# Own tiles for the first pairs' squares and key halves, another order of their factors, 24 turns of the identity, and a changed rule for when the planner lets loads follow each other

## The chip, the core and the metric

The kernel runs on one core of a Trainium2 chip. The time is in device microseconds (us) from start to end of one execution. Five instruction streams work at once: TensorE (PE in the profile, with its weight loads as PEld), VectorE (DVE), ScalarE (ACT), GpSimd (POOL) and SyncE (SP), which here only issues DMAs. Each runs its own instructions in the order in which the program lists them; they wait for each other at semaphores.

## What is computed

Attention with normalized queries and keys over 8 x 12 heads of 448 positions and 64 dimensions, and a two-layer product with a cosine between the layers on its output:

```python
def rmsnorm(x, g):
    rms = np.sqrt(np.mean(x * x, axis=-1, keepdims=True) + 1e-06)
    return x / rms * g
q_n, k_n = (rmsnorm(q, g_q), rmsnorm(k, g_k))
scores = scale * np.matmul(q_n, k_n.transpose(0, 1, 3, 2))
scores = scores - np.max(scores, axis=-1, keepdims=True)
attn = np.exp(scores)
attn = attn / (np.sum(attn, axis=-1, keepdims=True) + 1e-09)
attn_out = np.matmul(attn, v).astype(np.float32)
...
x = np.ascontiguousarray(attn_out.transpose(0, 2, 1, 3)).reshape(B * S, H * D)
h = x @ w_in          # 3584 x 768 by 768 x 2048
g = h * np.cos(h)
return (g @ w_out).astype(np.float32)
```

## The kernel before

The 96 heads are handled as 48 pairs `u`, two heads on the 128 partitions, and six pairs make one batch of 448 tokens (`NP = 6`, eight batches). For each pair the kernel computes the scores (`score`, L425), the row minimum (the sign of the scores is turned, `rowmin`, L443), the exponential with its row sums (`expo`, L453), transposes of the result on TensorE (`transp`, L480), and the product with the values (`av_whole` L516 for the first nine pairs, `av` L506 for the others). Four score tiles fit into PSUM for the first batch (three in ring `S`, one in `ph`). The hidden layer of a batch (`ffn1`, L564) is multiplied in among the attention of the next batch, and its result goes through SBUF tiles `he` (two of them) to a buffer `h_d` in DRAM (`h_out` L583, `h_store` L587).

The weights of the first layer come as 64-bit floats in 16 loads of 768 KB (`w_load`, L202). VectorE and ScalarE decode them (`decode`, L210), ScalarE and GpSimd split them into a high and a low part. The second layer's weights are decoded too, combined, and kept in DRAM as `wo_d`.

**The first two pairs** (`NFIRST = 2`) are prepared in a shorter way than the others (`first`, L737). The two halves of `sd` (queries `c = 0`, keys `c = 1`) are loaded (`first_load`, L309), squared on ScalarE into the PSUM tile `pt` (`first_square`, L313), summed on VectorE (`first_reduce`, L318) and raised to the power -1/2 on GpSimd (`st_pow`, L304). The keys are multiplied by their factor (`first_norm`, L326), turned on TensorE into `pt` (`first_turn`, L332), and copied into the tile `khi`, its upper half by ScalarE and its lower by VectorE (`first_keys`, L337). The queries are scaled by GpSimd with a constant that VectorE makes out of the small load `gs` (`q_scale` L382, `g_fold` L189), and their own factor is multiplied in by the row minimum (L449). `pt` is also what all transposes go through.

**What sets the order.** No engine's order is written by hand. Each step is handed to `Plan.add` with its engine, an assumed cost, a due time, what it reads and writes, for DMAs an assumed time `land` until the data is there, and sometimes an earliest time `start`. `Plan.order` (L69) runs a list scheduler over these assumed times: when an engine is free, it takes the step with the earliest due time among those that are ready. The result is one fixed list; on the chip each engine works through its part of it, whatever the real times are, and the assumed times are not waited for. Rings (`RING` L196, `RING2` L892) are tiles with several copies: the first user of copy n waits in the plan for all users of copy n - ring size, and (L73) for the first user of copy n - 1. If that first user is a DMA, the plan counts its cost, its `land` and a signal time of 0.16 before the next may start.

**The second part** (from L890) has a plan of its own. It starts with the hidden layer of the last batch in 16 blocks of 3.66 us (`ffn1_block`, L577), and beside it prepares the blocks of the second layer: `gl_load` (L593) loads two rows of `h_d` into `hb` (three copies), ScalarE and VectorE compute the cosine (L599 to L623), VectorE or GpSimd adds or subtracts blocks (`g_mix`, L625), ScalarE and GpSimd split them (`g_split`, L628), and TensorE multiplies them with the weights that `v_place` (L277) loads (`ffn2`, L637). For each of four pairs of batches there are 16 such blocks, in four groups g for each of the roles a, b, d, c; seven products follow in order, the first with a, the second with b (made of d and b).

Of the kernel before, what the change touches and what calls it, by code (L numbers as in the profile page):

```python
# [27 lines left out]
class Plan:  # L28
# [9 lines left out]
    def __init__(self, rings):  # L38
        self.rings = rings
        self.parts = []  # L40
        self.start = []
        self.lead = []
        self.writer = {}
        self.readers = {}
        self.users = {}

    def add(self, eng, cost, due, fn, *args, r=(), w=(), land=0.0, start=0.0, lead=None):
# [21 lines left out]
    def order(self):  # L69
        parts = self.parts  # L70
        for (name, inst), users in self.users.items():
            parts[users[0]][5].update(self.users.get((name, inst - self.rings[name]), ()))
            parts[users[0]][5].update(self.users.get((name, inst - 1), ())[:1])  # L73
            parts[users[0]][5].discard(users[0])
            for n in users[1:]:
                parts[n][5].add(users[0])
# [14 lines left out]
        while True:  # L91
            best = None
            for e in free:
                if can[e]:
                    t = free[e]
                elif wait[e]:
                    t = max(free[e], wait[e][0][0])
                else:
                    continue
                if best is None or t < best[0]:  # L100
                    best = (t, e)
            if best is None:
                break
            t, e = best
            while wait[e] and wait[e][0][0] <= t:
                n = heapq.heappop(wait[e])[1]
                heapq.heappush(can[e], (parts[n][2], n))
            n = heapq.heappop(can[e])[1]
            cost, fn, args, land = (parts[n][i] for i in (1, 3, 4, 6))
            end = free[e] = t + cost  # L110
            self.busy[e] += cost
            seq.append((t, n, fn, args))
            for m in after[n]:
                same = parts[m][0] == e and not land
                gap = 0.0 if same else land + self.SIGNAL + self.lead[m]
                ready[m] = max(ready[m], end + gap)
                left[m] -= 1
                if not left[m]:
                    heapq.heappush(wait[parts[m][0]], (ready[m], m))
# [7 lines left out]
def tile_attention_moe(  # L127
# [185 lines left out]
    def first_square(u, c):  # L313
        nc.scalar.activation(
            pt[:, 512 * (1 - c) : 512 * (1 - c) + S], pair[u][f"sd{c}"].rearrange("p t d -> p (t d)"), AF.Square
        )

    def first_reduce(u, c):  # L318
        if c:
            tl(u, "r", [128, 14], F32)  # L320
        src = pt[:, 512 * (1 - c) : 512 * (1 - c) + S].rearrange("p (t d) -> p t d", d=D)
        r = pair[u]["r"][:, 7 * c : 7 * c + 7]
        nc.vector.tensor_reduce(r, src, axis=AX.X, op=ALU.add)
        nc.vector.tensor_scalar(r, r, 1.0 / D, 1e-6, op0=ALU.mult, op1=ALU.add)  # L324

    def first_norm(u):  # L326
# [3 lines left out]
        del pair[u]["sd0"]  # L330

    def first_turn(u):  # L332
        kn = pair[u].pop("rkb")
        for t in range(7):
            nc.tensor.transpose(pt[:D, t * 128 : t * 128 + 128], kn[:, t * D : t * D + D], ident)

    def first_keys(u, hh):  # L337
        if hh == 0:
            tl(u, "khi", [128, S], F32)
        dst = pair[u]["khi"][64 * hh : 64 * hh + 64].rearrange("d (p t) -> d t p", t=7)  # L340
        src = pt[:D, :896].rearrange("d (t c) -> d t c", c=128)[:, :, 64 * hh : 64 * hh + 64]
        if hh == 0:
            nc.scalar.copy(dst, src)  # L343
        else:
            nc.vector.tensor_copy(dst, src)
# [79 lines left out]
    def score(u, j):  # L425
# [5 lines left out]
        for n, t in enumerate(tiles):  # L431
            tag = place(u, 2 * j + n)[0]
            pool = ps_h if tag == "ph" else ps_s
            d["S", t] = pool.tile([128, 512], F32, tag=tag, name=f"S{u}_{t}")
        for n, (a, c) in enumerate(ops):
            for t in tiles:
# [263 lines left out]
    def weights(fc):  # L700
        d = ffn_due(0, 3 * fc) - 6.0
        w, f = ("w", fc), ("wf", fc)
        begin = (4.0, 7.0, 20.0)[fc] if fc < 3 else max(24.0 + 7.0 * fc, d - WAHEAD)
        add(SP, ISS, d - 30.0, w_load, fc, w=[w if f64 else f], land=8.0, start=begin)
# [32 lines left out]
    def first(u):  # L737
        D0 = base(u) - 34.0
        add(SP, 2 * ISS, D0, first_load, u, w=[("P", 2 * u), ("P", 2 * u + 1)], land=2.6)
        for c in (1, 0):  # L740
            z = [("pt", 0, 1 - c)]
            add(ACT, 0.5, D0 + 2 - c, first_square, u, c, r=[("P", 2 * u + 1 - c)], w=z)
            add(DVE, 0.75, D0 + 3 - c, first_reduce, u, c, r=z, w=[("r", u, c)])
            add(POOL, 1.5, D0 + 4 - c, st_pow, u, 7 * c, 7 * c + 7, w=[("r", u, c)])
        add(DVE, 0.65, D0 + 5, first_norm, u, r=[("P", 2 * u), ("P", 2 * u + 1), ("r", u, 1)], w=[("rkb", u)])
        z = [("pt", 0, 0), ("pt", 0, 1)]
        add(PE, 1.2, D0 + 6, first_turn, u, r=[("rkb", u)], w=z, lead=0.0)
        add(ACT, 0.6, D0 + 7, first_keys, u, 0, r=z, w=[("khi", u, 0)])
        add(DVE, 0.65, D0 + 7, first_keys, u, 1, r=z + [("khi", u, 0)], w=[("khi", u, 1)])
        add(SP, ISS, D0 + 1, q_load, u, w=[("qd", u)], land=4.0)  # L750
        add(POOL, 0.8, D0 + 5, q_scale, u, r=[("gsc", 0), ("qd", u), ("r", u, 0)], w=[("qhi", u)])
        add(SP, ISS, base(u) - 6, v_whole, u, w=[("vs", u, 0)], land=LAND, start=14.0 + 6 * u)

    def prepare(u):
# [25 lines left out]
        for hh in range(2):  # L780
            vd, vs = [("vd", 2 * u + hh)], [("vs", u, hh)]
            add(SP, ISS, D0 - 12 + 6 * hh, v_load, u, hh, w=vd, land=LAND)
            add(POOL, 0.56, D0 + 6 * hh, v_high, u, hh, r=vd, w=vs)
            add(POOL, 0.91, D0 + 2 + 6 * hh, v_low, u, hh, r=vd, w=vs)

    def attend(u):
# [4 lines left out]
        for j in range(4):  # L791
# [4 lines left out]
            operands = ("qhi", "khi") if u in S32 else ("qhi", "ql", "khi", "kl")  # L796
            add(PE, cost, dj, score, u, j, lead=lead, r=[(n, u) for n in operands if u >= NFIRST or n != "khi"] + ([("khi", u, 0), ("khi", u, 1)] if u < NFIRST else []), w=keys)
            for t, key in zip(tiles, keys):
# [11 lines left out]
        for kc in range(4):  # L810
# [14 lines left out]
            for hh in range(2):  # L825
                n = 8 * u + 2 * kc + hh
                eng, cost = (DVE, 0.62) if u in A32 and hh and kc < 3 else (ACT, 0.53)
# [8 lines left out]
            if u in A32:  # L836
                n = 8 * u + 2 * kc
                add(PE, 1.0, dk + 4, av_whole, u, kc, lead=lead, r=[("vs", u, 0), ("hi", n), ("hi", n + 1)], w=[("O", u, 0)])
                continue
            for hh in range(2):  # L840
                n, m = 8 * u + 2 * kc + hh, 6 * u + 2 * kc + hh
                r = [[("hi", n), ("lo", m)], [("hi", n), ("lo", m)], [("lo", m)], [("hi", n), ("hi", n - 2)]][kc]
# [16 lines left out]
    def multiply(b):  # L859
        for fc in range(NFC):  # L860
# [7 lines left out]
            add(SP, ISS, d, h_store, b, fc, r=[("he", NFC * b + fc)], land=LAND)  # L868

    for u in range(NP):  # L870
        (first if u < NFIRST else prepare)(u)
# [191 lines left out]
```

## Time and profile before

| | |
|---|---|
| median of three runs | 1447.98 us (1443.79, 1447.98, 1448.81) |
| the profiled execution | 1448.93 us |
| its span, from the first to the last instruction | 1447.1 us |
| mean granted TensorE clock | 0.998 |
| HBM read, written | 218.24 MB, 62.89 MB |

Everything in the profile belongs to one execution; it ran 1.8 us longer than its span and 0.95 us longer than the median run. Where a row is a line of the time line, it gives start, duration, engine, line of the kernel, operation, output<-inputs and, in brackets, how long the engine had been idle and what ended that. In a row of the windows, each engine has its busy time and its number of instructions, then come the granted clock, the busy share of the DMA engines and GB/s. An fp32 product stands in the records as two matmul instructions.

### The profile page before, as it was taken

What the parts mean: (1) busy time and instruction counts of PE and PEld (TensorE: products, weight loads), DVE (VectorE), ACT (ScalarE), POOL (GpSimd) and SP (SyncE); (2) the same over time, 40 slices, a digit from 0 to 9 for tenths busy, and PEclk for the clock granted to TensorE, in tenths of its full rate; (3) what the DMA queues carried; (4) which work ended last, traced back from release to release, by engine and by line L of the source; (5) the groups of instructions that cost most, each with busy time, mean ns of one, the idle gap of its engine ahead of it and who ended that gap; (6) DMA issues with size and microseconds to landing.
All of it is one profiled execution on the core that took longest, in us unless ns stands there. A gap on an engine that the chain in (4) does not pass through costs nothing.

```text
span 1447.1 us, 22426 instructions
## 1 busy us (share of the span) xinstructions
PE 1397.0 (97%) x7361; PEld 1152.7 (80%) x7361; DVE 1020.8 (71%) x1649; ACT 1001.6 (69%) x2058; POOL 932.6 (64%) x722
## 2 busy tenths in 40 slices
PE   6999999999999999999999999999999999999998
PEld 2445687888888788787878788889889899899898
DVE  6878885677778777869676755536876876977821
ACT  5777677677777777777776676547676776786742
POOL 5678777566877867787884673101295596585684
PEclk9999999999999999999999999999999999999999
DMA  6788444555667576566654542149569569489373
GB/s 207 230 259 255 129 129 133 151 175 173 192 200 222 166 219 206 185 206 188 215 184 159 163 149 87 55 132 347 195 201 327 188 224 338 154 265 339 124 238 101
DMA packets 154452, 282.62 MB, mean 195 GB/s; under 512 B 31760, under 2 KB 102368, under 8 KB 154336
## 3 DMA queue, kind: packets, MB, share of 16 engines
q1 hardware_dynamic: 154336, 281.20, 60.7%
q8 instruction: 58, 0.95, 0.3%
q14 instruction: 58, 0.48, 0.1%
HBM read 218.24 MB, written 62.89 MB: 194 GB/s over the span
## 4 chain that ended last, share of the span: by engine, by line
PE 71%; DVE 14%; ACT 5%; DMA 4%; issue 4%; POOL 2%; SPq 0%; ACTq 0%; DVEq 0%; POOLq 0%
PE ph L573 9%; PE PT L483 8%; PE ph L574 8%; PE ph L575 8%; PE O L514 8%; PE S L438 7%; PE y L649 7%; PE y L650 7%; PE y L648 7%; DVE lo L502 2%; DMA hb<-h_d 2%; ACT hi L494 1%; POOL glo L633 1%; DVE sm L447 1%; PE O L522 1%
## 5 line engine op out<-in xcount | busy, mean ns | idle before, releaser
L573 PE MATMUL ph<-xs,wi 128*128 128x448 f32 x768 | 299.2, 390 | 1.5 <-ACT he L585 1.5
L574 PE MATMUL ph<-xs,wi 128*128 128x448 f32 x768 | 281.1, 366 | 0.0
L575 PE MATMUL ph<-xs,wi 128*128 128x448 f32 x768 | 281.0, 366 | 0.0
L456 ACT ACTIVATE P<-S,sm 128x448 f32<-128x448 f32 x336 | 213.7, 640 | 78.7 <-DVE sm L447 66.6
L649 PE MATMUL y<-glo,wo 128*128 128x448 f32 x672 | 247.1, 368 | 7.3 <-POOL glo L633 7.3
L648 PE MATMUL y<-ghi,wo 128*128 128x448 f32 x672 | 246.8, 367 | 0.3 <-ACT ghi L635 0.3
L650 PE MATMUL y<-ghi,wo 128*128 128x448 f32 x672 | 246.7, 367 | 0.0
L494 ACT CAST hi<-PT 128x448 fp32r<-128x448 f32 x312 | 153.5, 536 | 93.9 <-PE PT L483 49.6
L447 DVE TENSOR_REDUCE sm<-S 128x1 f32<-128x448 f32 x322 | 186.7, 611 | 25.6 <-PE S L438 24.9
L483 PEld LDWEIGHTS PT<-ident,P 128*128 128x128 f32 x1344 | 155.5, 141 | 41.6 <-issue 22.8
L502 DVE TENSOR_TENSOR lo<-PT,hi 128x448 fp32r<-128x448 f32 x234 | 134.7, 617 | 71.5 <-ACT hi L494 70.2
L483 PE MATMUL PT<-ident,P 128*128 128x128 f32 x1344 | 181.2, 275 | 3.0 <-DVE hi L492 3.0
L573 PEld LDWEIGHTS ph<-xs,wi 128*128 128x128 f32 x768 | 144.5, 188 | 34.9 <-issue 15.7
L575 PEld LDWEIGHTS ph<-xs,wi 128*128 128x128 f32 x768 | 144.2, 188 | 12.6
L574 PEld LDWEIGHTS ph<-xs,wi 128*128 128x128 f32 x768 | 144.9, 189 | 9.7 <-issue 0.4
L649 PEld LDWEIGHTS y<-glo,wo 128*128 128x128 f32 x672 | 126.6, 188 | 19.4 <-POOL glo L633 8.7
L306 POOL TENSOR_TENSOR r<-r,nhalf 128x14 f32<-128x14 f32 (+1 forms) x50 | 128.5, 2570 | 12.5 <-DVE r L324 8.9
L648 PEld LDWEIGHTS y<-ghi,wo 128*128 128x128 f32 x672 | 126.6, 188 | 11.7 <-ACT ghi L635 0.7
L650 PEld LDWEIGHTS y<-ghi,wo 128*128 128x128 f32 x672 | 126.6, 188 | 10.9
L438 PE MATMUL S<-khi,qhi 64*128 64x448 f32 x399 | 115.0, 518 | 1.7 <-ACT khi L343 1.2
L514 PE MATMUL O<-hi,vs 128*128 128x448 f32 x312 | 101.9, 381 | 7.3 <-ACT hi L494 3.3
L514 PE MATMUL O<-lo,vs 128*128 128x448 f32 x234 | 89.3, 397 | 10.3 <-DVE lo L502 9.8
(225 smaller groups left out, 2710.7 us busy)
## 6 DMA issues: line engine op xcount, KB each, us to landing
wo<-wo_d SPq DMA_DIRECT2D x88, 768.0 KB
h_d<-he SPq DMA_DIRECT2D x128, 224.0 KB
hb<-h_d SPq DMA_DIRECT2D x64, 448.0 KB
wo_d<-wv SPq DMA_DIRECT2D x56, 384.0 KB
sd<-sd SPq DMA_DIRECT2D x46, 448.0 KB
vd<-v SPq DMA_DIRECT2D x78, 160.0 KB
qd<-qT SPq DMA_DIRECT2D x48, 256.0 KB
raw<-w_in SPq DMA_DIRECT2D x16, 768.0 KB
```

The lines of the kernel that those rows point to most:

```text
L438: nc.tensor.matmul(d["S", t][:, :S], d[a][p0:p1, j * 128 : j * 128 + 128], d[c][p0:p1, :], start=(n == 0), stop=(n == len(ops) - 1),)
L447: nc.vector.tensor_reduce(least, d["S", t][:, :S], axis=AX.X, op=ALU.min)
L456: nc.scalar.activation(tl(u, f"P{t}", [128, S], F32, "P"), d.pop(("S", t))[:, :S], AF.Exp, bias=sm[:, 1, t : t + 1], scale=-1.0, accum_out ...
L483: nc.tensor.transpose(pt[:, t * 128 : t * 128 + 128], src, ident)
L494: nc.scalar.copy(hi, pt[:, hh * S : hh * S + S])
L514: nc.tensor.matmul(O, st, d.pop((what, kb, hh)), start=(kc + n == 0), stop=(kc + n == 4))
L573: nc.tensor.matmul(ph[:, :S], whi, x2[:, 0, :], start=(cc == 0), stop=False)
L574: nc.tensor.matmul(ph[:, :S], whi, x2[:, 1, :], start=False, stop=False)
L575: nc.tensor.matmul(ph[:, :S], wlo, x2[:, 0, :], start=False, stop=(cc == NCC - 1))
L648: nc.tensor.matmul(y, whi, hi, start=(k == 0 and chain < 2), stop=False, skip_group_check=chain == 2)
L649: nc.tensor.matmul(y, whi, lo, start=False, stop=False, skip_group_check=chain == 2)
L650: nc.tensor.matmul(y, wlo, hi, start=False, stop=(k == NH - 1), skip_group_check=chain == 2)
```

## The change

- Squares: `first_square` writes a tile of ring `hi` (four copies) in SBUF rather than a half of `pt`; the numbers of later `hi` tiles move up by four.
- Key halves: the upper half is copied into a tile of `khi`, the lower into a tile of ring `kl`, and the second copy no longer follows the first. `score` for the first two pairs multiplies by halves; the middle query tile (t = 3) becomes two products of 64 rows and 64 columns.
- Factors: the keys' `st_pow` is due earlier, that of the queries 20 us after the pair's start; `q_scale` no longer comes after the queries' factor.
- `warm`: 24 transposes of the identity into `pt`, on TensorE, ready from 1.0 us of the plan.
- Loads: the first two weight loads may start at 9 and 13 us of the plan (4 and 7 before); a value load of a pair from 9 on not more than 60 us ahead of the pair.
- Planner: where the first user of copy n waits only for the first user of copy n - 1, and both are on the same engine, the landing of the first one's data is no longer counted. This holds for both plans.

```diff
@@ Plan.order
-            parts[users[0]][5].update(self.users.get((name, inst - 1), ())[:1])
+            old = self.users.get((name, inst - 1))
+            if old and old[0] not in parts[users[0]][5]:
+                parts[users[0]][5].add(old[0])
+                self.issue.add((old[0], users[0]))
...
-                same = parts[m][0] == e and not land
+                same = parts[m][0] == e and (not land or (n, m) in self.issue)
@@ first_square, first_reduce
-        nc.scalar.activation(
-            pt[:, 512 * (1 - c) : 512 * (1 - c) + S], pair[u][f"sd{c}"].rearrange("p t d -> p (t d)"), AF.Square
-        )
+        nc.scalar.activation(tl(u, f"sq{c}", [128, S], F32, "hi"), pair[u][f"sd{c}"].rearrange("p t d -> p (t d)"), AF.Square)
...
-        src = pt[:, 512 * (1 - c) : 512 * (1 - c) + S].rearrange("p (t d) -> p t d", d=D)
+        src = pair[u].pop(f"sq{c}").rearrange("p (t d) -> p t d", d=D)
@@
+    def warm():
+        for n in range(24):
+            nc.tensor.transpose(pt[:, 128 * (n % 7) : 128 * (n % 7) + 128], ident, ident)
@@ first_keys
-        if hh == 0:
-            tl(u, "khi", [128, S], F32)
-        dst = pair[u]["khi"][64 * hh : 64 * hh + 64].rearrange("d (p t) -> d t p", t=7)
+        k = tl(u, f"k{hh}", [128, S], F32, ("khi", "kl")[hh])
+        dst = k[64 * hh : 64 * hh + 64].rearrange("d (p t) -> d t p", t=7)
@@ score
+        if u < NFIRST:
+            for t in tiles:
+                for hh in (0, 1) if t == 3 else (t // 4,):
+                    p, m = 64 * hh, slice(64 * hh, 64 * hh + 64) if t == 3 else slice(0, 128)
+                    q = d["qhi"][p : p + 64, j * 128 : j * 128 + 128]
+                    nc.tensor.matmul(d["S", t][m, :S], q[:, m], d[f"k{hh}"][p : p + 64, :], start=True, stop=True)
+            return
@@ weights
-        begin = (4.0, 7.0, 20.0)[fc] if fc < 3 else max(24.0 + 7.0 * fc, d - WAHEAD)
+        begin = (9.0, 13.0, 20.0)[fc] if fc < 3 else max(24.0 + 7.0 * fc, d - WAHEAD)
@@ first
-            z = [("pt", 0, 1 - c)]
-            add(ACT, 0.5, D0 + 2 - c, first_square, u, c, r=[("P", 2 * u + 1 - c)], w=z)
-            add(DVE, 0.75, D0 + 3 - c, first_reduce, u, c, r=z, w=[("r", u, c)])
-            add(POOL, 1.5, D0 + 4 - c, st_pow, u, 7 * c, 7 * c + 7, w=[("r", u, c)])
+            sq = [("hi", 2 * u + 1 - c)]
+            add(ACT, 0.55, D0 + 2 - c, first_square, u, c, r=[("P", 2 * u + 1 - c)], w=sq)
+            add(DVE, 0.75, D0 + 3 - c, first_reduce, u, c, r=sq, w=[("r", u, c)])
+            add(POOL, 1.5, D0 + 3 if c else D0 + 20, st_pow, u, 7 * c, 7 * c + 7, w=[("r", u, c)])
...
-        add(PE, 1.2, D0 + 6, first_turn, u, r=[("rkb", u)], w=z, lead=0.0)
-        add(ACT, 0.6, D0 + 7, first_keys, u, 0, r=z, w=[("khi", u, 0)])
-        add(DVE, 0.65, D0 + 7, first_keys, u, 1, r=z + [("khi", u, 0)], w=[("khi", u, 1)])
+        add(PE, 1.0, D0 + 6, first_turn, u, r=[("rkb", u)], w=z, lead=0.0)
+        for hh, eng in ((0, ACT), (1, DVE)):
+            add(eng, 0.95, D0 + 7, first_keys, u, hh, r=z, w=[(("khi", "kl")[hh], u, hh)])
...
-        add(POOL, 0.8, D0 + 5, q_scale, u, r=[("gsc", 0), ("qd", u), ("r", u, 0)], w=[("qhi", u)])
+        add(POOL, 0.8, D0 + 5, q_scale, u, r=[("gsc", 0), ("qd", u)], w=[("qhi", u)])
@@ prepare
-            add(SP, ISS, D0 - 12 + 6 * hh, v_load, u, hh, w=vd, land=LAND)
+            add(SP, ISS, D0 - 12 + 6 * hh, v_load, u, hh, w=vd, land=LAND, start=D0 - 60)
@@
+    add(PE, 5.0, -40.0, warm, w=[("pt", 0, 0), ("pt", 0, 1)], start=1.0)
```

More of the change, by code (lines that the diff above doesn't have):

```diff
@@ L45, in __init__ @@
         self.users = {}
+        self.issue = set()
     def add(self, eng, cost, due, fn, *args, r=(), w=(), land=0.0, start=0.0, lead=None):
@@ L796, in attend @@
             operands = ("qhi", "khi") if u in S32 else ("qhi", "ql", "khi", "kl")
-            add(PE, cost, dj, score, u, j, lead=lead, r=[(n, u) for n in operands if u >= NFIRST or n != "khi"] + ([("khi", u, 0), ("khi", u, 1)] if u < NFIRST else []), w=keys)
+            add(PE, cost, dj, score, u, j, lead=lead, r=[(n, u) for n in operands if u >= NFIRST or n != "khi"] + ([("khi", u, 0), ("kl", u, 1)] if u < NFIRST else []), w=keys)
             for t, key in zip(tiles, keys):
@@ L825, in attend @@
             for hh in range(2):
-                n = 8 * u + 2 * kc + hh
+                n = 2 * NFIRST + 8 * u + 2 * kc + hh
                 eng, cost = (DVE, 0.62) if u in A32 and hh and kc < 3 else (ACT, 0.53)
@@ L836, in attend @@
             if u in A32:
-                n = 8 * u + 2 * kc
+                n = 2 * NFIRST + 8 * u + 2 * kc
                 add(PE, 1.0, dk + 4, av_whole, u, kc, lead=lead, r=[("vs", u, 0), ("hi", n), ("hi", n + 1)], w=[("O", u, 0)])
@@ L840, in attend @@
             for hh in range(2):
-                n, m = 8 * u + 2 * kc + hh, 6 * u + 2 * kc + hh
+                n, m = 2 * NFIRST + 8 * u + 2 * kc + hh, 6 * u + 2 * kc + hh
                 r = [[("hi", n), ("lo", m)], [("hi", n), ("lo", m)], [("lo", m)], [("hi", n), ("hi", n - 2)]][kc]
```

## The prediction

> **What bounds the kernel now.** I read the page's busy lines and chain first, then the windows (busy time per engine in a stretch), then the time line where TensorE idles.
>
> ```profile
> span 1447.1 us, 22426 instructions
> PE 1397.0 (97%) x7361; PEld 1152.7 (80%) x7361; DVE 1020.8 (71%) x1649; ACT 1001.6 (69%) x2058; POOL 932.6 (64%) x722
> PE 71%; DVE 14%; ACT 5%; DMA 4%; issue 4%; POOL 2%; SPq 0%; ACTq 0%; DVEq 0%; POOLq 0%
> ```
>
> TensorE is the bound: 97% busy, and 71% of the chain. All but a handful of its products stay, so the change can win only what TensorE loses to idling (1447.1 - 1397.0 = 50 us in all, in many places) or to a slow clock. Two stretches matter. The first is the start:
>
> ```profile
> 3.54 1.19 ACT L314 ACTIVATE PT<-sd 128x448 f32<-128x448 f32 x2 [1.54 <-DMA sd<-sd]
> 4.77 0.62 DVE L323 TENSOR_REDUCE r<-PT 128x7 f32<-128x448 f32 x1 [3.89 <-ACT PT L314]
> 5.68 2.96 POOL L306 TENSOR_TENSOR r<-r,nhalf 128x7 f32<-128x7 f32 x2 [4.39 <-DVE r L324]
> 7.22 0.63 DVE L329 TENSOR_TENSOR rkb<-sd,r 128x448 f32<-128x448 f32 x1 [0.89 <-POOL r L306]
> 7.99 1.68 PE L335 MATMUL PT<-ident,rkb 128*64 128x128 f32 x7 [7.99 <-DVE rkb L329]
> 8.06 0.95 ACT L295 ACTIVATE sd<-sd 128x896 f32<-128x896 f32 x1 [3.32 <-DMA sd<-sd]
> 8.29 0.16 DVE L190 SCALAR_TENSOR_TENSOR gs<-gs 128x1 f32<-128x1 f32 x1 [0.45 <-DMA gs<-gg]
> 10.73 0.95 DVE L345 COPY khi<-PT 64x448 f32<-64x448 f32 x1 [2.28 <-ACT khi L343]
> 10.84 4.25 PE L438 MATMUL S<-khi,qhi 64*128 64x448 f32 x8 [1.18 <-ACT khi L343]
> 14.34 1.08 DVE L298 TENSOR_REDUCE r<-sd 128x14 f32<-128x896 f32 x1
> 15.87 0.69 DVE L449 TENSOR_SCALAR_CACHE_REDUCE S<-S,r 128x448 f32<-128x448 f32 x1
> 16.65 0.63 ACT L456 ACTIVATE P<-S,sm 128x448 f32<-128x448 f32 x1 [3.81 <-DVE S L449]
> 19.84 0.56 DVE L216 TENSOR_SCALAR wf<-raw 128x768 int32<-128x768 int32 x1
> ```
>
> A chain of single steps leads to the first scores at 10.84. Yet the first row minimum runs only at 15.87: VectorE's queue holds pair 1's preparation ahead of it, and that had to wait for `pt`.
>
> The second stretch is the second product of the second part (loads of `hb`, then ACT, DVE, POOL, PE, then windows):
>
> ```profile
> 953.95 0.43 SPq L596 DMA_DIRECT2D hb<-h_d  x1
> 966.90 0.42 SPq L596 DMA_DIRECT2D hb<-h_d  x1
> 1008.22 0.38 SPq L596 DMA_DIRECT2D hb<-h_d  x1
> 1026.33 30.76 SPq L596 DMA_DIRECT2D hb<-h_d  x5
> 1015.70 0.55 ACT L601 ACTIVATE n0b<-hb 128x448 int32<-128x448 f32 x1 [1.00 <-DMA hb<-h_d]
> 1025.68 0.61 DVE L623 TENSOR_TENSOR B0b<-c0b,hb 128x448 f32<-128x448 f32 x1
> 1045.88 1.09 DVE L626 TENSOR_TENSOR B0b<-B0d,B0b 128x896 f32<-128x896 f32 x1
> 1048.10 3.00 POOL L633 TENSOR_TENSOR glo<-B0b,ghi 128x896 fp32r<-128x896 f32 x1 [5.46 <-ACT ghi L635]
> 1051.16 0.47 PE L649 MATMUL y<-glo,wo 128*128 128x448 f32 x1 [2.61 <-POOL glo L633]
> 985.00:995.00 10.00, 10.00 (x50) 9.09 (x49) 5.78 (x10) 8.03 (x15) 2.88 (x2) 1.00 1.02 355
> 1035.00:1045.00 10.00, 10.00 (x50) 9.09 (x49) 9.90 (x12) 5.82 (x10) 3.36 (x2) 1.00 0.16 46
> 1045.00:1055.00 10.00, 7.04 (x26) 5.81 (x25) 9.90 (x12) 6.59 (x10) 6.90 (x3) 0.83 0.14 46
> ```
>
> TensorE is full until 1047 and then waits for the low part of b's last group, because VectorE, 58% busy at 985 to 995, runs at 99% from 1035: its work came late. In that last window TensorE is busy 7.0 of 10 us and its clock is 0.83: 3.0 us idle and 0.17 x 10 = 1.7 us of clock. The modelled ends of its products hide a little more idling, and I put the stall at 5.0 us.
>
> **The change part by part, and the sum.**
>
> *Squares in own tiles.* The first sum starts at 4.77, when both squares are done (3.54 + 1.19 = 4.73), though it needs only the first (about 4.1). Gain 0.6 us, if nothing else comes before it.
>
> *Pair 1's loads earlier.* By the planner's new rule both halves of pair 1 are issued straight behind the first q load, where the 448 KB load of pair 2 stood, and take its place in the DMA queue. That load had landed at 8.06 (ScalarE's square of it). So the halves land, I estimate, at about 7.1 and 8.0. In the plan (landing assumed after 2.6 us) pair 1's two sums are ready just before the keys' factor of pair 0, at 6.3 against 6.9 by the plan's costs, so they stand ahead of `first_norm` in VectorE's queue. On the chip this is a new wait: squares until 8.7, the second sum until 9.3, its scaling 0.17, `first_norm` at 9.6 instead of 7.22. Behind it wait the turn, both copies, and everything on TensorE.
>
> *gs and q.* `gs` now lands behind another 448 KB, at about 9.5 instead of 8.2; GpSimd runs pair 1's and the queries' powers (1.48 each, half of 2.96) before `q_scale`, which ends near 12.3. It hides under the next step, by 0.7 us.
>
> *Key halves.* Turn 10.3 to 12.0 (1.68), then both copies side by side until 13.0 (0.95 once, where it was twice). First scores at 13.1: 2.3 us later than 10.84.
>
> *Row minima.* Behind the copies VectorE has pair 1's norm (0.63) and pair 2's sum (1.08, which waits for ScalarE's 0.95 square at 13.0): the first row minimum starts at 15.1, 0.8 earlier. Pair 1's keys are then turned between pair 0's scores, and from the fourth exponential on I count 0.6 to 1 us earlier. **The start gives -1.0 us.** Bounds: +2.3 (the delay of the first scores goes through) and -3.8 (ScalarE's whole wait before its first exponential, the row at 16.65).
>
> *Middle query tile.* Two products of 64 rows and 64 columns instead of one of 128.
>
> ```profile
> 25.53 1.02 PE L438 MATMUL S<-khi,qhi 64*128 64x448 f32 x4
> 44.96 1.02 PE L438 MATMUL S<-khi,qhi 128*128 128x448 f32 x2 [0.30 <-ACT P L456]
> ```
>
> Two products on different halves take as long as one on all rows, 1.02 us. So zero, at most 2 x 1.02 if the two do not overlap.
>
> *Later loads of weights, later value load.* SP does not wait for the plan's times.
>
> ```profile
> 4.95 1.58 SPq L205 DMA_DIRECT2D raw<-w_in  x2
> ```
>
> The first weight load stays close to its 4.95, and the second moves behind pair 1's q load, to about 12.4. The first decoding stands at 19.84, 13 us behind the end of these issues, so 6 to 7 us of cover are left: zero. Without the cover the decoding would meet row minima (0.69 each), 1 us or so.
>
> *24 turns of the identity.* They run on an idle TensorE from 1.4 us on and end near 7 (24 x 0.24, from 1.68 / 7), before the first turn: no cost. What they could win is a faster clock.
>
> ```profile
> L438 PE MATMUL S<-khi,qhi 64*128 64x448 f32 x8 | 4.2, 987 | 1.2 <-ACT khi L343 1.2
> L438 PE MATMUL S<-khi,qhi 64*128 64x448 f32 x28 | 7.2, 588 | 0.0
> 174.78:178.20 3.42, 3.42 (x16) 2.78 (x13) 2.12 (x4) 1.89 (x3) 2.23 (x3) 0.55 0.40 122
> 176.03 1.70 PE L483 MATMUL PT<-ident,P 128*128 128x128 f32 x7
> ```
>
> The first row is from 10 to 16 us, the second from 30 to 60: the first scores take 987 ns instead of 588, so TensorE runs slow there (the clock column, 1.00 at the start, has no record before the first change). After a stall the clock fell near 174.4 and was back about 3.4 us later, though half of that time (1.70) went to transposes: transposes seem to count. But here TensorE idles from 7 to 10.3, about as long as the pause that slowed it before 1051.16. So I count zero.
>
> The Trainium skill says otherwise of the cause ("TensorE: Matmul & The Clock Gate", Part 4): transposes do not raise the clock, as they are not counted as busy in the same way. By that rule the sum is the same, and the case further down in which the warm clock lasts has no chance at all; the row at 174.78 speaks against the rule.
>
> *The planner's rule in the second part.* The first three loads of `hb` may now follow each other; the second came 13 us after the first (953.95, 966.90). After these, the three buffers set the pace: one is loaded and used from 1008.22 to 1026.3 (the row at 1025.68), 18 us, a third of which is 6.0, and the loads from 1008.22 to 1026.33 came 6.0 us apart. So the pace stays and only the head start remains. The first buffer's line gains nothing; I put the two others, with the last block needed, at 3 to 6 us, as ScalarE and VectorE still take one block after the other. The last sum of d and b (1045.88 + 1.09) needs 4.2 us to reach TensorE, and must be 3.6 us earlier to cause no wait. That is inside 3 to 6, and VectorE has the room (5.78 of 10). **I take the stall as gone: -5.0 us.** Bounds: 0 and -5.0. SP's order moves too: the loads are put ahead of `v_place` and `h_store`.
>
> Sum: -1.0 - 5.0 = -6.0 us on the profiled execution's 1448.9: 1442.9. That execution ran 0.95 above the median of the runs, so against 1447.98 I say **1442.0 us**.
>
> **The rivals.**
>
> *The stall stays* (28%). The head start is eaten by the single PSUM tile between ACT and DVE, or VectorE's sums meet GpSimd's subtractions (3.00 at 1048.10). Speaking for it: the pace does not change. Then only the start counts: 1447.
>
> *The new order also ends the third stall* (15%).
>
> ```profile
> 169.21 1.92 DVE L220 SCALAR_TENSOR_TENSOR wf<-raw,wf 128x768 int32<-128x768 int32 x1
> 172.58 0.44 PE L514 MATMUL O<-hi,vs 128*128 128x448 f32 x1 [2.65 <-ACT hi L494]
> ```
>
> VectorE decodes weights while TensorE waits 2.65 us, and the slow clock after it (0.55 over 3.42) costs 0.45 x 3.42 = 1.5: 4.2 us. Every list changes, so this may vanish; it may as well return elsewhere. 1442.0 - 4.2 = 1437.8.
>
> *Slower* (12%): SP's queue in the second part. A load of `hb` that waits for its buffer holds the stores of `he` behind it; `he` has two tiles, so ScalarE stops, and the banks for product 0 come late.
>
> ```profile
> L649 PEld LDWEIGHTS y<-glo,wo x672: 186/188/334, 1021.5 to 1442.5; 128*128 128x128 f32 x168
> 1018.71 0.53 ACT L585 COPY he<-ph 128x448 f32<-128x448 f32 x1
> 1023.47 0.54 ACT L585 COPY he<-ph 128x448 f32<-128x448 f32 x1 [1.88 <-DMA h_d<-he]
> ```
>
> Product 0 starts at 1021.5 (the first start in the first row) and needs the copy of 1018.71, finished 2.3 us before. From a lag of 2.3 us on, each microsecond costs one, and past some 3 us of idling 1.7 for the clock. A lag of 13 us, two buffer waits of 6, costs 10.7 + 1.7 and leaves no stall to win: 1447.98 - 1.0 - 5.0 + 12.4 = 1454; with a smaller lag 1449 to 1454.
>
> *The warm clock lasts* (3%): if it survives the pause, the turn takes half of 1.68 and the first scores 588 / 987 of their time: 0.8 + 1.7. 1439.5.
>
> **How the numbers follow.** A measurement of this kernel tells about 0.5% from no change, 7.2 us: below 1440.7 or above 1455.2. The forecast (42%) runs from 1439 to 1445. Faster: 0.3 of it, nearly all of the 15% and the 3%: 0.30. Slower: under half of the slower rival: 0.05. The rest, 0.65, is no difference. The range leaves out the outer part of the slower rival and the lowest of the case at 1437.8: 1436 to 1450.
>
> **What would show it.** Start: `first_norm` near 9.6, first scores near 13, first row minimum near 15; if `first_norm` is at 6.6, I have the queue wrong. Clock: the first turn still 1.68. Second part: the second and third load of `hb` right behind the first, TensorE's window at 1045 full, clock 1.00. The prediction is wrong if the stall near 1047 remains, if a new wait of TensorE over 3 us appears at the start of product 0, or if new stalls arise in the first 180 us.

## The result, and the profile after

| | before | after |
|---|---|---|
| median of seven runs each | 1447.98 us (1443.23 to 1448.81) | 1454.28 us (1451.04 to 1457.39) |
| ratio, 95% interval | | 1.0057 [1.0040, 1.0074] |
| the profiled execution, its span | 1448.93, 1447.1 us | 1457.39, 1455.4 us |
| mean granted clock | 0.998 | 0.992 |

The kernel became slower by 0.57%, 12 us from the forecast and above the range. The two mean clocks do not compare: the record of the clock begins with its first change, at 24.3 us in before and at 5.9 in after, and what lies ahead of it counts as 1.00. The lines of the kernel after are 2 to 13 higher. First its page (span, busy lines, chain):

```profile
span 1455.4 us, 22505 instructions
PE 1408.8 (97%) x7389; PEld 1158.7 (80%) x7389; DVE 1027.5 (71%) x1649; ACT 1000.9 (69%) x2058; POOL 922.8 (63%) x722
PE 71%; DVE 7%; issue 3%; ACT 3%; POOL 2%; DMA 1%; SPq 0%; ACTq 0%; POOLq 0%; DVEq 0%
```

TensorE is the bound as before; VectorE's share of the chain went from 14% to 7%, and yet the time rose. The time line of after shows the start (start, duration, then the operation):

```profile
9.22 0.62 DVE L331 TENSOR_TENSOR rkb<-sd,r 128x448 f32<-128x448 f32 x1
9.90 1.70 PE L341 MATMUL PT<-ident,rkb 128*64 128x128 f32 x7 [3.54 <-DVE rkb L331]
11.63 0.95 ACT L348 COPY k<-PT 64x448 f32<-64x448 f32 x1 [3.19 <-PE PT L341]
12.62 0.95 DVE L350 COPY k<-PT 64x448 f32<-64x448 f32 x1 [2.71 <-ACT k L348]
12.73 2.75 PE L445 MATMUL S<-k,qhi 64*128 64x448 f32 x4 [1.14 <-ACT k L348]
15.14 0.68 DVE L461 TENSOR_SCALAR_CACHE_REDUCE S<-S,r 128x448 f32<-128x448 f32 x1
18.14 0.96 DVE L350 COPY k<-PT 64x448 f32<-64x448 f32 x1 [2.26 <-ACT k L348]
18.95 0.67 DVE L461 TENSOR_SCALAR_CACHE_REDUCE S<-S,r 128x448 f32<-128x448 f32 x1
30.72 0.97 PE L445 MATMUL S<-k,qhi 64*64 64x448 f32 x4
34.13 1.36 DVE L220 TENSOR_SCALAR wf<-raw 128x768 int32<-128x768 int32 x1
35.53 1.64 DVE L222 SCALAR_TENSOR_TENSOR wf<-raw,wf 128x768 int32<-128x768 int32 x1
60.66 0.60 DVE L544 TENSOR_TENSOR xf<-O,rs 128x448 f32<-128x448 f32 x1
```

Up to the first row minimum (15.14) the steps come within 0.6 us of where the prediction has them. Then VectorE stands 2.26 us in front of pair 1's key copy (0.42 us in before), which is next in its queue, while pair 0's other row minima wait behind it (second at 18.95, before 16.47). Pair 0 ends as before (`x_out` at 45.5 in both), pair 1 does not: 60.66, 4.5 us later than this row of before:

```profile
56.15 0.61 DVE L532 TENSOR_TENSOR xf<-O,rs 128x448 f32<-128x448 f32 x1
```

The waits of TensorE from 10 to 60 us (in total, times, longest) name VectorE, first before, then after:

```profile
PE O L522 <- DVE hi L492: 1.4, 1, 1.4
PE PT L483 <- DVE hi L492: 1.0, 2, 0.6
```

```profile
PE O L534 <- DVE hi L504: 2.4, 2, 1.3
PE PT L495 <- DVE hi L504: 1.5, 2, 1.1
```

Part of VectorE's work also takes longer in this execution: the decoding step at 34.13 has 1.36 us where the same step had 0.56 in before (19.84), and GpSimd's operations run beside it from 34.07 on:

```profile
34.07 2.29 POOL L243 TENSOR_TENSOR wi<-wf,wi 128x384 fp32r<-128x384 f32 x2 [1.81 <-ACT wi L238]
```

That the two hold each other up is how I read it. After's other steps of this kind agree: up to 190 us the eight that run alone or beside a power on GpSimd (L310) take 0.54 to 0.56 us, and the five that start while GpSimd runs a split or a product take 0.77 to 1.49. Up to the end of pair 1 the decoding takes 3.9 us more than its steps take undisturbed, 1.5 us more in before. The windows of two stretches of 100 us (PE busy and, as x, its instructions) show the rest, before and after:

```profile
60.00:160.00 100.00, 94.82 (x473) 52.85 (x472) 82.77 (x123) 73.68 (x166) 77.43 (x57) 1.00 0.82 251
160.00:260.00 100.00, 94.51 (x524) 76.39 (x523) 77.58 (x119) 72.76 (x164) 75.18 (x67) 0.98 0.41 125
```

```profile
60.00:160.00 100.00, 90.93 (x426) 47.46 (x424) 78.91 (x117) 70.68 (x160) 65.28 (x50) 0.97 0.75 239
160.00:260.00 100.00, 95.69 (x527) 76.42 (x527) 76.41 (x117) 70.59 (x156) 70.95 (x63) 0.98 0.44 131
```

From 60 to 160 us TensorE has done 47 instructions fewer, at some 0.2 us each 9.4 us, and in the next 100 us it keeps pace. Clock 0.97 there is 3 us of it. The second part then starts 9.7 us late (1021.5 before):

```profile
L661 PEld LDWEIGHTS y<-glo,wo x672: 186/188/330, 1031.2 to 1450.7; 128*128 128x128 f32 x168
```

Its products take 419.5 us from first to last (1031.2 to 1450.7), against 421.0 in before. The wait at 1047 is gone, but a smaller one stands at 1065, again with slow clock:

```profile
1045.00:1055.00 10.00, 10.00 (x50) 9.07 (x50) 9.90 (x10) 6.60 (x11) 4.82 (x3) 1.00 0.32 92
1055.00:1065.00 10.00, 10.00 (x49) 8.77 (x47) 9.88 (x12) 5.98 (x10) 7.10 (x3) 1.00 0.14 45
1065.00:1075.00 10.00, 7.90 (x31) 6.99 (x31) 5.34 (x9) 9.04 (x15) 9.79 (x6) 0.83 0.61 196
```

So in this execution the first part lost 9.7 us and the second won 1.5 instead of 5.0. It is the slowest of the seven, 3.1 us above their median; how much of the 9.7 belongs to the list is told below (a_no_turns).

### The profile page after: what moved, and what is told of

Same layout as the page of the kernel before. It is cut to its first block, busy times and chain, and to the rows that moved or that the text cites. A ratio compares the mean times of both kernels' runs of the same rounds, so it can differ in the third digit from the quotient of the medians.

```text
span 1455.4 us, 22505 instructions
## 1 busy us (share of the span) xinstructions
PE 1408.8 (97%) x7389; PEld 1158.7 (80%) x7389; DVE 1027.5 (71%) x1649; ACT 1000.9 (69%) x2058; POOL 922.8 (63%) x722
## 4 chain that ended last, share of the span: by engine, by line
PE 71%; DVE 7%; issue 3%; ACT 3%; POOL 2%; DMA 1%; SPq 0%; ACTq 0%; POOLq 0%; DVEq 0%
PE ph L585 9%; PE ph L586 8%; PE ph L587 8%; PE y L661 8%; PE y L662 8%; PE y L660 8%; PE O L526 8%; PE PT L495 7%; PE S L450 6%; DVE lo L514 2%; POOL glo L645 1%; ACT hi L506 1%; DVE B0b L638 1%; DVE sm L459 1%; DVE xf L557 1%
## 5 line engine op out<-in xcount | busy, mean ns | idle before, releaser
L587 PEld LDWEIGHTS ph<-xs,wi 128*128 128x128 f32 x768 | 144.8, 189 | 12.7
L310 POOL TENSOR_TENSOR r<-r,nhalf 128x14 f32<-128x14 f32 (+1 forms) x50 | 126.4, 2529 | 9.5 <-DVE r L326 5.7
L450 PE MATMUL S<-khi,qhi 64*128 64x448 f32 (+1 forms) x371 | 101.8, 491 | 0.6 <-ACT P L468 0.6
```

Of the source, the lines that this page charges most:

```text
L450: nc.tensor.matmul(d["S", t][:, :S], d[a][p0:p1, j * 128 : j * 128 + 128], d[c][p0:p1, :], start=(n == 0), stop=(n == len(ops) - 1),)
L587: nc.tensor.matmul(ph[:, :S], wlo, x2[:, 0, :], start=False, stop=(cc == NCC - 1))
```

## The experiments

Theory A: parts of the change cost at the start (late loads of weights, the new rule putting pair 1 ahead, turns), and the 4.5 us at pair 1 are carried on. Theory B: any edit that touches the planner's input makes its greedy scheduler build another list, and lists differ by more than the parts are worth. The planner keeps the time at which each engine's list ends by the costs written in the kernel (`self.end`); TensorE's is called the **count**. It is no time of the chip, only what the scheduler believes. All runs, with the start of pair 1's `x_out` and of the first product of the second part in the profiled execution:

| run | count, part 1 | part 2 | pair 1 | product 0 | median us | ratio to before, 95% |
|---|---|---|---|---|---|---|
| before | 950.4 | 472.6 | 56.2 | 1021.5 | 1446.3 to 1447.0 | |
| after | 956.8 | 469.0 | 60.7 | 1031.2 | 1454.28 | 1.0057 [1.0040, 1.0074] |
| b_rule_second | 950.4 | 469.0 | 55.8 | 1021.6 | 1450.31 | 1.0019 [1.0000, 1.0037] |
| b_late_weights | 950.4 | 472.6 | 55.8 | 1022.2 | 1449.33 | 1.0014 [0.9993, 1.0034] |
| a_no_turns | 956.8 | 469.0 | 60.2 | 1026.1 | 1453.74 | 1.0042 [1.0023, 1.0060] |
| b_signal_017 | 947.9 | 479.4 | 57.3 | 1017.2 | 1452.55 | 1.0042 [1.0022, 1.0062] |
| a_land_499 | 947.4 | 469.0 | 59.6 | 1020.6 | 1446.89 | 1.0007 [0.9989, 1.0025] |
| a_land_503 | 941.9 | 468.9 | 60.6 | 1021.1 | 1444.10 | 0.9987 [0.9968, 1.0006] |
| a_rule_second | 948.5 | 469.0 | 57.8 | 1019.5 | 1449.83 | 1.0019 [1.0001, 1.0038] |
| a_early_weights | 951.7 | 469.0 | 58.1 | 1023.7 | 1446.78 | 0.9997 [0.9979, 1.0016] |
| b_signal_014 | 936.9 | 469.5 | 55.6 | 1008.5 | 1438.04 | 0.9934 [0.9911, 0.9958] |
| a_signal_013 | 935.4 | 468.6 | 60.5 | 1020.9 | 1452.22 | 1.0042 [1.0026, 1.0058] |
| b_signal_018 | 954.2 | 484.0 | 55.0 | 1028.4 | 1462.82 | 1.0117 [1.0094, 1.0139] |
| a_turns_50 | 956.8 | 469.0 | 60.6 | 1026.3 | 1453.63 | 1.0046 [1.0031, 1.0061] |
| a_013_turns_50 | 935.4 | 468.6 | 56.9 | 1017.6 | 1448.46 | 1.0016 [0.9999, 1.0034] |
| a_signal_014 | 940.7 | 468.9 | 58.8 | 1013.4 | 1446.02 | 0.9982 [0.9960, 1.0004] |

Runs with b_ are before with one edit, those with a_ after with one. The medians are of 7 to 12 runs, of six in b_signal_014 and b_signal_018. The medians of before are those of the four sets in which the runs were timed; after's own ratio is against the 1447.98 of the first table. Pair 1 and product 0 are from one execution each. TensorE's own order in the second part is the same in all sixteen kernels; only the other engines' order differs there.

### One part of the change alone, or undone

**The rule in the second part alone** (`Plan` gets a switch that is on for the second plan):

```diff
-                self.issue.add((old[0], users[0]))
+                if self.follow:
+                    self.issue.add((old[0], users[0]))
...
-    plan = Plan(RING2)
+    plan = Plan(RING2, True)
```

> The kernel before with the planner's new rule for the second part alone; the first part's order is that of before. If the second part's step of the prediction holds and the loss sits in the first part: the first part ends when it does in before, TensorE's wait near 1047 is gone, and the time is 1443 to 1446 us (-5.0 where no new wait arises, -2.0 where the one that after shows from 1061 to 1094 belongs to the new list itself). If the new rule costs in the second part as well: 1448 or more.

Measured 1450.31: neither gain, and if anything 0.2% slower. Product 0 starts at 1021.6 as it should. The windows of this run:

```profile
1045.00:1055.00 10.00, 10.00 (x50) 8.99 (x48) 9.90 (x12) 5.99 (x9) 7.11 (x3) 1.00 0.09 25
1055.00:1065.00 10.00, 7.74 (x37) 6.68 (x36) 5.98 (x11) 9.88 (x17) 10.00 (x6) 1.00 0.67 246
1135.00:1145.00 10.00, 7.89 (x38) 7.00 (x39) 9.57 (x12) 8.73 (x15) 7.16 (x4) 1.00 0.39 120
```

The wait at 1047 is gone, and the second product, in which it stood, ends 4.9 us earlier (the third starts at 1051.6, in before at 1056.5). But TensorE waits 2.3 us at 1055 and 2.1 at 1135 instead, and the products take 421.0 us as they did:

```profile
L655 PEld LDWEIGHTS y<-glo,wo x672: 186/188/330, 1021.6 to 1442.6; 128*128 128x128 f32 x168
```

**Later loads of weights alone** (before with `begin = (9.0, 13.0, 20.0)[fc]`):

> The kernel before with the later times for the first loads of weights (9 and 13 instead of 4 and 7) alone. In the issue order only the second load of weights moves, behind pair 1's load of q. If later loads of weights are what pushes VectorE's decoding among the row minima: 1452 to 1458 us, with the first decoding at 23 us instead of 19.84. Rival, as the prediction had it (the load's cover of 6 to 7 us holds): 1447 to 1449 us.

1449.33, no difference that can be told; pair 1 is not late (55.8). Late loads as such are not the cause. This run says something else too: its second part has the very list of before, and yet there is little of before's stall (7.04 busy, clock 0.83) in the same window. A stall of that size stands 100 us later (in before these two windows have 10.00 and 8.59 busy, clock 1.00):

```profile
1045.00:1055.00 10.00, 8.86 (x44) 7.83 (x43) 9.90 (x12) 6.88 (x10) 8.30 (x3) 1.00 0.15 46
1145.00:1155.00 10.00, 7.42 (x36) 6.33 (x34) 9.90 (x11) 7.90 (x13) 3.54 (x3) 1.00 0.14 48
1155.00:1165.00 10.00, 9.98 (x41) 9.02 (x42) 8.03 (x13) 6.31 (x11) 10.00 (x4) 0.83 0.14 47
```

At 1047 that is about 1.1 us of idling and no slow clock, where I had put 5.0. The products take 421.8 us all the same (421.0 in before): where the stall stands is a matter of the execution, and a gain at one place does not add to the whole.

**Without the turns** (the line that adds `warm` removed; all lists else are those of after):

> After without the 24 turns of the constant; every engine's order is otherwise that of after. If the turns cost nothing and win nothing: 1453 to 1455 us, first scores at 12.7 us and the first turn 1.70 us as in after. If they delay the first turn or heat the clock's control: 1449 to 1452. If they bring the clock up earlier later on (it was back at 19.5 in after and 24.3 in before): 1456 or more, and the clock is back only near 24.

1453.74, as after: the turns cost nothing and win nothing. The first turn takes 1.70 us as expected; the first scores come at 11.94, 0.8 us earlier than expected, and the clock is up from 16.3 to 19.7 us and again from 26.5. As it has after's list, it also shows what of after's profile is the list's: pair 1 is 4.0 us late and product 0 4.6, not 9.7. The decoding step that took 1.36 us in after takes 0.54 here (at 34.44), and pair 1 is late all the same. The window from 60 to 160 us has clock 1.00 here and 0.97 in after's profiled execution:

```profile
60.00:160.00 100.00, 91.65 (x444) 48.43 (x442) 82.38 (x123) 72.37 (x165) 67.05 (x53) 1.00 0.77 245
```

### An edit of nothing

**The planner's assumed signal latency** in before, `SIGNAL = 0.17` for 0.16:

> The kernel before with the latency that its planner assumes for a signal at 0.17 instead of 0.16 us: no instruction is added or taken away, but the order of most lists changes a little. If the time follows from named steps alone: 1447 to 1449 us. If any other order of the lists moves waits about by itself: 3 us or more away from 1448 on either side, with the lag gathered in other places than in after.

1452.55: an edit that changes no instruction costs 0.42%, about as much as the whole change (0.57%). The first part ends 4.3 us earlier than in before, the second (1017.2 to 1447.2) takes 430.0 us instead of 421.0. Theory A has no place for that.

### The change with other lists

**The assumed landing of loads in after**: `ISS, LAND = 0.45, 4.99`, then `5.03`, for 5.0.

> After with one number of the planner changed, the landing that it assumes for most loads: 4.99 instead of 5.00 us. Nothing is added or taken away, and the issue order of every engine is that of after up to the fourth pair or so. Theory A, the loss comes from the start (VectorE's wait at 15.74 us and the decoding among the row minima, +4.5 us at pair 1): 1453 to 1456 us, pair 1's x_out at 60.7 us and the first part's end as late as in after. Theory B, the loss is the length of the one list that the greedy planner happened to build: by the planner's own count of its costs the first list ends at 947.4 instead of 956.8 (before: 950.4), so 1445 to 1449 us, although pair 1's x_out is as late as in after.

> After with 5.03 us for the same number; the order is that of after up to the third pair or so. Theory A: 1453 to 1456 us. Theory B: the planner's count for the first list is 941.9, so 1439 to 1444 us and the first product of the second part starts about 10 us earlier than in a run of after.

1446.89, as theory B gave, and 1444.10, 0.1 us above what it gave. Every part of the change is in both, their start is in the order of after, and pair 1 is as late (59.6, 60.6). But product 0 starts 10.6 and 10.1 us earlier than in after's profile, 5.5 and 5.0 earlier than without the turns. Where, the windows of the run with 4.99 show:

```profile
60.00:160.00 100.00, 92.70 (x453) 50.58 (x454) 80.59 (x118) 71.97 (x161) 70.51 (x54) 0.98 0.78 247
160.00:260.00 100.00, 100.00 (x565) 80.88 (x563) 80.60 (x126) 75.96 (x172) 77.39 (x71) 1.00 0.44 130
```

From 160 to 260 us TensorE has no gap at all and does 41 instructions more than before (565 for 524), 38 more than after. Theory A, which had 1453 to 1456 here, falls.

The planner's own times tell where after's list is long. Pair 1's `x_out` stands in them at 57.8 us for after and at 57.7 for before, so the count knows nothing of pair 1's delay. TensorE's gaps between 60 and 215 us of the plan add up to 19.3 us in after's list and to 12.7 in before's. On the chip both come together. Measured by the planned cost of the steps that TensorE has begun, a_no_turns is 2.6 us behind before at 60 us, 8.3 at 215 and 4.9 at 930; the run with 4.99 is 2.2 us behind at 60, 1.7 at 215 and 1.9 ahead at 260.

**The rule undone in the first part, the times of the weights undone** (both in after; the switch above, and `(4.0, 7.0, 20.0)`):

> After with the planner's new rule for the second part alone; the first part is ordered by the old rule, with all other edits of after. If the new rule in the first part (pair 1's loads ahead, and all that follows) is the cause by itself: 1446 to 1449 us, while both runs with another landing stay at 1454. Theory B: the planner's count is 948.5, so 1446 to 1449 us here too, but the runs with another landing move as well. If neither: 1453 or more.

> After with the old times for the first loads of weights (4 and 7). Late weights as the cause: 1446 us or less, with the first decoding near 20 us. Theory B: the planner's count for the first list is 951.7, 5 below after, so 1448 to 1451 us. Neither: 1454.

1449.83 and 1446.78, the first 0.8 us above what was expected of either theory, the second 1.2 below what B gave. Taken alone, each would look like the guilty part. Next to the runs with other landings they say only that all four other lists are faster than after's. Pair 1 comes 2 to 3 us earlier than in the profiles of after's list, so both parts seem to have a share in its delay.

### Does the count tell the time?

**Short and long counts** (`SIGNAL = 0.14` and `0.18` in before, `0.13` in after):

> The kernel before with the planner's latency of a signal at 0.14 instead of 0.16 us, and nothing else. The planner's own count is 936.9 for the first list (before 950.4) and 469.5 for the second (472.6). Theory B (the length of the list that happens to be built): 1433 to 1441 us, most of it gained before the first product of the second part, which starts near 1010 instead of 1021.5. If the count does not tell the time and each list is a draw of its own: anywhere from 1443 to 1455.

> The kernel before with 0.18 us for the same latency. The planner's count is 954.2 and 484.0 (before 950.4 and 472.6). Theory B: slower than before and than after, 1456 to 1463 us, and the loss in the second part, whose products take 425 us or more from first to last instead of 421. If the count does not tell the time: 1443 to 1455, the spread of the lists seen.

> After with the planner's latency of a signal at 0.13 instead of 0.16 us, and nothing else. The planner's count is 935.4 and 468.6 (after: 956.8 and 469.0). Theory B: 1433 to 1441 us, all parts of the change kept. If a part of the change costs by itself, whatever the list: 1447 or more.

The first two came as expected: 1438.04, faster than both kernels, with product 0 at 1008.5, and 1462.82, the slowest, with 427.3 us for the second part's products (1028.4 to 1455.7). But the count of the second part alone tells little: with 0.14 it is 469.5, 3.1 below before, and the products take 426.5 us (1008.5 to 1435.0), 5.5 more. Pair 1 stands at 55.6 and 55.0, so nothing of these 25 us is decided at the start. The third is a miss: 1452.22. Its start differs from that of the run with 4.99 by the clock (the column behind POOL's), which stays low longer in these profiles of one execution each. First the run with 0.13, then the one with 4.99:

```profile
10.00:20.00 10.00, 8.49 (x23) 4.13 (x24) 5.00 (x9) 3.16 (x5) 7.36 (x7) 0.50 0.46 173
20.00:30.00 10.00, 9.98 (x26) 3.40 (x25) 8.05 (x22) 6.98 (x19) 1.34 (x2) 0.59 0.87 233
```

```profile
10.00:20.00 10.00, 8.19 (x23) 3.51 (x21) 5.42 (x11) 3.74 (x7) 6.58 (x6) 0.60 0.59 213
20.00:30.00 10.00, 9.23 (x30) 3.08 (x31) 9.12 (x24) 7.92 (x23) 3.24 (x3) 0.83 0.87 237
```

**More turns** (`range(50)` for `range(24)`), first in after, then in the run that missed; the lists stay the same:

> After with 50 turns of the constant instead of 24; every list is that of after. The turns should end near 9.6 us, right before the first turn of keys at 9.9. If the clock fell in after because TensorE then stood still from 6.36 to 9.90 us: the first turn takes 0.85 instead of 1.70 us and the first scores 588 instead of 987 ns, so the first exponential comes 1 to 2 us earlier. If turns of a constant don't hold the clock: 1.70 us again. The whole time: 1454 as after if the start's gains are lost in the first 200 us (theory B), 1452 if they last.

> After with the latency of a signal at 0.13 us and 50 turns of the constant instead of 24; the lists are those of the run with 0.13 and 24 turns. If its late start under the slow clock (0.5 from 7.7 us for 20.48 us) is what spoiled that list: the first turn takes 0.85 to 0.95 us instead of 1.70, pair 0's x_out comes 2 us earlier (45.5 instead of 47.8), and the time is 1446 to 1449 us. If the start's delay is soaked up later, as elsewhere: 1450 to 1453 us, no change.

In after they change nothing (1453.63; the first exponential comes at 17.56 instead of 17.90, not 1 to 2 us earlier); in the other they win 3.8 us (1448.46; the intervals of the two ratios, 1.0026 to 1.0058 and 0.9999 to 1.0034, still overlap). Both time lines:

```profile
1.34 8.13 PE L336 MATMUL PT<-ident 128*128 128x128 f32 x50 [1.34 <-POOL ident masks.py:199]
10.30 0.95 PE L341 MATMUL PT<-ident,rkb 128*64 128x128 f32 x7 [0.83 <-DVE rkb L331]
15.08 1.70 PE L341 MATMUL PT<-ident,rkb 128*64 128x128 f32 x7
```

```profile
9.63 0.93 PE L341 MATMUL PT<-ident,rkb 128*64 128x128 f32 x7
12.00 1.59 PE L445 MATMUL S<-k,qhi 64*128 64x448 f32 x4 [1.45 <-POOL qhi L388]
13.53 1.39 PE L341 MATMUL PT<-ident,rkb 128*64 128x128 f32 x7
```

The first turn of keys takes half the time in both (0.95 and 0.93 for 1.70). After that the clock falls again in the one (1.70 at 15.08) and mostly holds in the other (1.39 at 13.53), and there pair 0's `x_out` comes at 43.5 instead of 47.8. With the same list this lead is carried on: 3.6 us at pair 1, 3.3 at product 0. So a delay at the start can count within a list, if these two profiles stand for their runs.

**A second list of after with a short count** (`SIGNAL = 0.14`):

> After with the planner's latency of a signal at 0.14 us instead of 0.16, and nothing else. The planner's count is 940.7 and 468.9, close to the run with landings of 5.03 (941.9 and 468.9), which took 1444. If the count tells the time for lists of after too, and the one at 0.13 is a single miss: 1441 to 1447 us. If the edits of the change cost something in every list planned with shorter latencies: 1450 or more.

1446.02, as the count gave. The list at 0.13 stays the one miss; the slow start explains some 3.8 us of it, and the rest (1448.5 where its count asked for 1441 or less) is open.

Over all sixteen kernels the correlation of the two counts' sum with the median is 0.71, and 0.92 without the two at 0.13, which were left out after they had missed; some of the sixteen share a list. The four lists of before that differ only in latency (0.14, 0.16, 0.17, 0.18) have a mean of 1450, the five of after (0.13, 0.14, 0.16 and the two landings) one of 1449: the change by itself makes no difference that these lists show. As the four lie up to 25 us apart, an effect of a few us either way could hide in this.

## Why the prediction was wrong

- **The start, -1.0 us: wrong.** `first_norm` (9.22 for 9.6), the cold turn (1.70 for 1.68), the first scores (12.73 for 13.1) and the first row minimum (15.14 for 15.1) were right. Two things were not. The copies do not run side by side: VectorE's still waits for ScalarE's (2.71 at 12.62), though the plan no longer asks for it; why, no run tells. That the first row minimum came on time is partly luck: the copy ended at 13.57, not 13.0, but pair 2's sum then had nothing left to wait for. And behind the first row minimum I had no wait: there stands pair 1's key copy, which costs 2.26 us, so that pair 0's first four exponentials come 1.2 us later than in before (17.90 for 16.65 the first, 21.05 for 19.83 the fourth) and only the last three 0.3 to 1.2 earlier; then the decoding meets the copies for pair 0's product. Pair 0 ended at 45.5 as before, so 0.0 in place of -1.0; pair 1 was 4.0 to 4.5 us late in the three profiles of after's list.
- **Later loads, zero: right as far as the loads go** (b_late_weights); where the planner then puts the decoding I had not costed, and that this is a cost is read from the trace alone.
- **The middle query tile and the turns, zero: right** (a_no_turns for the turns). The tile's two half products run side by side: 0.97 us for both (the row at 30.72), 1.02 for the one on all rows.
- **The second part, -5.0 us: the stall went, the gain did not come.** With the rule alone the second product ended 4.9 us earlier, and the products took 421.0 us as before; in after it made up 5.0 us of the 9.7, and the wait at 1065 took back 3.9. The step that failed is that nothing else would wait: I took TensorE to be full but for that stall. It is not, and time won at one product is given back at the next waits. And 5.0 was the size of that wait in one execution; b_late_weights has 1.1 there.
- **The term that failed most is one that I had left out.** I wrote that every list changes, and used it only for a rival that gains. The first part between the start and product 0 was taken as unchanged; with the lists tried here it moves product 0 by -13.0 to +6.9 us (b_signal_014, b_signal_018) without any real edit. After's list came out long (count 956.8, before 950.4): it loses further between 60 and 215 us, where other lists with the same start make pair 1's delay good, and ends 4.6 to 4.8 us late at product 0 (a_no_turns, a_turns_50; 9.7 in after's own profile). This term I had at zero. The range should have reached some 12 us to both sides for that alone, since the medians of the four lists of before run from 1438 to 1463.
- The rival that ended slower (SP's queue ahead of product 0) did not happen: the lag is 9.7 us at the last `x_norm` of the first part and at product 0.
- That the warm clock lasts had 3%: in after it did not (up from 5.9 to 9.3 us, and the turn at 9.90 took 1.70). The Trainium skill ("TensorE: Matmul & The Clock Gate", Part 4) says that transposes do not raise the clock. The runs disagree: in a_turns_50 turns alone ran until 9.5 us, their spacing fell from 213 to 109 ns near 6.3 us, and the turn of keys behind them took 0.95 us instead of 1.70.
- One line of the section on the change is wrong: the keys' `st_pow` is due 3 us after the pair's start in both kernels; only that of the queries moved, from 4 to 20.

Shown by runs: that after's time is a matter of its list, and that no part of the change is needed for such a loss. Only read from the trace: that VectorE's wait at 18.14 and the decoding among the row minima make up the 4 us at pair 1; the slowed steps can be but a small part, as a_no_turns has 2.6 us of such slowing (before 1.5). Not settled: how pair 1's delay and the list's own gaps share the 4.6 us at product 0, and the list at 0.13.

## What to carry to other kernels

Where a greedy scheduler makes the order, an edit is measured together with a new draw of the whole order; here a draw is worth up to 12 us to either side, more than the edit. So time an edit under several draws (a latency off by 0.01 will do) before it is kept or blamed, widen the range by that scatter, and use the scheduler's own count to pick lists worth timing: that gave 1438.04 us, 0.66% faster than before, without an edit of the work, but it also missed once (0.13). A wait that goes is a gain only if the engine behind it has no other wait within the same period.

## What the runs showed of the hardware

**Two paces of TensorE.** In stretches without a gap and at full clock, products of 448 columns come at two steady rates. Before, then after, in the same windows of 60 us:

```profile
1180.00:1240.00 60.00, 60.00 (x298) 55.60 (x297) 42.66 (x67) 43.81 (x65) 38.06 (x19) 1.00 0.94 325
1300.00:1360.00 60.00, 60.00 (x298) 55.60 (x297) 44.50 (x66) 43.85 (x67) 35.18 (x16) 1.00 0.81 280
```

```profile
1180.00:1240.00 60.00, 60.00 (x292) 54.51 (x291) 43.99 (x73) 43.23 (x64) 38.86 (x19) 1.00 0.93 315
1300.00:1360.00 60.00, 60.00 (x293) 54.49 (x292) 46.73 (x71) 44.28 (x67) 35.41 (x17) 1.00 0.88 299
```

A window also counts the products at its edges; from start to start the trace has 202.7 ns on average in before and 206.7 in after, 4.0 ns for each product, 8.1 us over the 2016 (3 x 672) of the second part. In the five profiles compared (before, after, b_rule_second, b_late_weights, a_no_turns), the pace changes only where TensorE has had a gap, be it a short one. With the faster one come more gaps (before the products with `glo` the trace counts 8.4 us of idling in b_rule_second and 2.8 in after), and the second part comes out nearly the same. What sets the pace, no run tells.

**The scatter of one kernel.** 35 runs of before in one set lay between 1441.53 and 1453.99 us, and their mean clock between 0.992 and 0.999: the twelve at 0.998 averaged 1444.8, the seven below 0.995 1450.4. In this set the clock and the time have a correlation of -0.76, in the three others of -0.42 to -0.48. A single profiled execution can hold several us that the next one doesn't.
